# Four attention layers: which score banks VectorE takes over from ScalarE, by quota or by backlog

## The chip, the cores and the metric

The kernel runs on one core of one Trainium2 chip. The time is device microseconds of one execution; the number to compare is the median of several runs. Profiles are single executions taken by the hardware profiler, and a profile's times are measured from the first instruction of its span.

## What is computed

Four layers in a row on x of 2048 positions by 640 features, all bf16. Layers 0 and 2 use the weights A and attend to a sliding window of 256 positions; layers 1 and 3 use the weights B and attend to all 2048 positions. There are 32 heads of 20 features.

```python
x = x + A(layernorm(x)); x = x + B(layernorm(x))     # layers 0, 1
x = x + A(layernorm(x)); x = x + B(layernorm(x))     # layers 2, 3
# A, B: qkv = x @ wqkv; p = softmax(q k^T / sqrt(20)) (A: only 0 <= i - j < 256)
#       return (p v) @ wo
```

## The kernel before

**Units and banks.** The queries come in 4 chunks of 512 positions, the heads in 8 groups of 4. A unit is one layer, one chunk, one group (class Unit, L696). A full-attention unit has 16 key blocks of 128 times 4 heads, 64 score banks; a bank is a 128 x 512 block of scores (keys by queries) in one PSUM bank. A windowed unit has 12 banks. The first chunk of layer 1 is cut into parts of 4 key blocks, that of layer 3 into one of 12 and one of 4 (PARTS), since the last keys of a layer exist only when the layer before it is done. The list `units` (L752 on) fixes the order: layer 0 with the parts of layer 1's first chunk woven in; then layer 1's chunks 1 to 3 with the windowed units of layer 2's chunks 0 to 2 between them; then layer 3's first chunk, 12 key blocks a unit, with the windowed units of layer 2's last chunk after its fourth unit; then the 4 remaining key blocks of that chunk, 16 banks a unit; then layer 3's chunks 1 to 3.

**The main loop** (from L1323) goes tile by tile. A tile is 3 banks, sometimes 2 or 4, held alternately in PSUM banks 0 to 2 and 3 to 6. TensorE computes its scores (L1359), ScalarE takes the exponential of the whole tile in one instruction (L1387) and writes it to `pt` in SBUF; two or three tiles later TensorE multiplies it by the values into PSUM bank 7 (L1420). At a unit's end VectorE copies bank 7 out (finish_unit, L861; copies at L869, L871, L883, L885), and a tail task normalizes it (t_tail, L1065). In windowed units masks are multiplied in by VectorE (L1474) and by GpSimd (L1463).

**Background tasks** (layer norm, projections, output projection, tails) are generators in an ordered list. pump() advances them by a credit for each tile. They use PSUM banks 5 and 6, later bank 6 alone (take_m, L273); a task in the midst of a bank holds it (`state["held"]`). When TensorE would have too little to do, keep_clock (L663) adds filler matmuls on the masks (L307).

**VectorE's own exponentials.** Some score banks are not given to ScalarE. VectorE turns them into exponentials by arithmetic on the bits of the number. The bank is read from PSUM into a 32-bit integer form (side_fixed, L947; instruction L957). Two such banks make a pair, for which t_chain (L965) issues four more VectorE instructions (L969, L978, L980, L982). There are two buffers `xi` for the integer form, and three (layer 1) or five (layer 3) for the result, which stay taken until TensorE has multiplied the pair by the values (side_values, L1004; matmul L1010). In layer 1 these buffers lie in `raw_o` (side_early, L919), in layer 3 in buffers of the normalized input `xnT` and in `ka` and `qa` (side_start, L906).

Which banks are put aside is fixed when the units are made (put_aside, L683): in layers 1 and 3 from chunk 1 on, the last banks of each unit, 4 in layer 1, 6 or 8 by turns in layer 3, 4 in the very last unit, none in unit (3, 1, 0). In layer 1 a moved bank sits as the third bank of a tile, at fixed places written into the list `tiles` before the loop starts (L1252 to L1277), so that tile gives ScalarE 2 banks. In layer 3 it goes to PSUM bank 6 beside a full tile (side_scores, L937; scores L944), when `side_now` says so: no task holds bank 6, the bookkept backlog is under LAG = 0.5, the unit that the bank belongs to was loaded at least 8 tiles ago.

**The backlog.** `state["lag"]` is a running account, in microseconds, of the work issued to VectorE and not yet done: each VectorE operation adds a written-down cost (0.6 for a copy out of PSUM in evac, 1.2 in stats, 0.7 for L957, 0.7, 0.7, 1.2 and 1.2 for the steps of a chain), and each tile takes off its columns divided by 1200, plus 0.05 (L1447), that is 1.33 for 3 banks and 0.90 for 2. After each tile, side_work (L990) issues further steps of the chains while the account is under WORK = 1.0. Where a unit ends before its pairs are done, side_done (L1030) forces the steps out.

Of the kernel before, what the change touches and what calls it, by code (L numbers as in the profile page):

```python
# [23 lines left out]
NT = S // P  # L24
# [15 lines left out]
LAG = 0.5  # L40
WORK = 1.0
SIDE_1 = 4
SIDE_3 = (6, 8)
# [9 lines left out]
def kernel(  # L53
# [272 lines left out]
    def evac(out_, in_):  # L326
        if state["act"]:
            nc.scalar.copy(out=out_, in_=in_)
        else:
            state["lag"] += 0.6  # L330
            nc.vector.tensor_copy(out=out_, in_=in_)  # L331
# [60 lines left out]
    def stats(l, c, i):  # L392
        if (l, c) not in mvs:
            mvs[l, c] = lnp.tile([P, 4, 2], F32, name="mv", tag="mv")
        state["lag"] += 1.2
        st = lnp.tile([P, 2, 6], F32, name="stats", tag="stats")
        xv = x_sb[:, 4 * c + i, :]
        nc.vector.bn_stats(out=st[:, 0, :], in_=xv[:, 0:HD])
        nc.vector.bn_stats(out=st[:, 1, :], in_=xv[:, HD:D])
        nc.vector.bn_aggr(out=mvs[l, c][:, i, :], in_=st[:])  # L400
# [282 lines left out]
    def put_aside(l, c, g):  # L683

        if l == 1:
            n = SIDE_1
        else:
            n = 4 if (c, g) == (NC - 1, G - 1) else SIDE_3[g % 2]
        if n == 2:
            return ((NT - 1, 2), (NT - 1, 3))  # L690
        return tuple((NT - 1 - i // 4, i % 4) for i in range(n))

# [3 lines left out]
    class Unit:  # L696
        def __init__(self, l, c, g, part=None):
            self.l, self.c, self.g, self.part = l, c, g, part
            self.windowed = l % 2 == 0
            self.aside = ()  # L700
            if self.windowed:
                sets = [(m, b0, subs, j) for m, b0, subs in window_banks(c) for j in range(4)]
            else:

                if c > 0 and (l, c, g) != (3, 1, 0):
                    self.aside = put_aside(l, c, g)
                k0, k1 = key_blocks(l, part)
                sets = [
                    (None, 0, [(kc, 0, 4, 0)], j) for kc in range(k0, k1) for j in range(4)
                    if (kc, j) not in self.aside  # L710
                ]
            n = len(sets)
            self.banks = [
                (self, j, m, b0, subs, i < 4, i >= n - 4 + len(self.aside), i == n - 1)
                for i, (m, b0, subs, j) in enumerate(sets)
            ]
# [144 lines left out]
    def finish_unit(u):  # L861
# [31 lines left out]
    side_todo = deque(  # L893
        (u, p, i) for u in units for p in range(len(u.aside) // 2) for i in range(2)
    )
    side_left = Counter({id(u): len(u.aside) for u in units})
    side_out = {}
    side = {"xi": deque(), "chain": deque(), "out": deque(), "late": False}
# [7 lines left out]
    def side_start():  # L906

        assert live["xnT"] == 0 and not side["chain"] 
        tl = [xtp.tile([P, KD, C], BF16, name="xnT", tag="xnT") for _ in range(3)]
        live["xnT"] += 3  # L910
        f = [v[:, 0:4, :].rearrange("p a b -> p (a b)").bitcast(F32) for v in tl]
        side["xi"].clear()
        side["out"].clear()
        outs = [ka_all[:, KA - 6 + 2 * n : KA - 4 + 2 * n, :] for n in range(3)]
        outs += [qa_all[:, 2 * n : 2 * n + 2, :] for n in range(2)]
        side_tiles(f[0:2], f[2].bitcast(F16)[:, 0 : 2 * C], outs)
        side["late"] = True
# [9 lines left out]
    def side_free():  # L927

        if not side_todo or not side["late"]:
            return False  # L930
        u, p, i = side_todo[0]
        return (
            id(u) in loaded and state["tick"] >= loaded[id(u)] + 8
            and mfree[6][0] <= state["tick"] and (i == 1 or len(side["xi"]) > 0)
        )

    def side_scores():  # L937

        u, p, i = side_todo[0]
        mseq[0] += 1  # L940
        mfree[6] = (state["tick"] + 2, mseq[0])
        kc, j = u.aside[2 * p + i]
# [4 lines left out]
    def side_fixed(z):  # L947

        u, p, i = side_todo.popleft()
        side_left[id(u)] -= 1  # L950
        if not side_left[id(u)] and id(u) in deferred:
            live["kt"] -= 1
            live["qt"] -= 1
        if i == 0:
            side["now"] = side["xi"].popleft()
        xi = side["now"]
# [33 lines left out]
    def side_work(force):  # L990

        while (force or state["lag"] < WORK) and side["chain"]:
# [11 lines left out]
    def side_values(u, pairs, done):  # L1004

        for n in range(done, len(pairs)):
            pt = pairs[n][0]
            for i in range(2):
                kc, j = u.aside[2 * n + i]
                nc.tensor.matmul(  # L1010
                    op[32 * j : 32 * j + VW, :], lhsT=u.v(kc, j), rhs=pt[:, i, :], start=False,
                    stop=all(jj != j for _, jj in u.aside[2 * n + i + 1 :]),
                    skip_group_check=True,
                )
            side["out"].append(pt)

    def side_push():
# [3 lines left out]
        if side_free():  # L1021
            side_scores()
# [7 lines left out]
    def side_done(u):  # L1030

        n = 0
        while len(side_out.get(id(u), ())) < len(u.aside) // 2:
            n += 1
            assert n < 10000
            side_push()
        return side_out.pop(id(u))
# [5 lines left out]

    def s_emitted(u):
# [6 lines left out]
        elif side_left[id(u)]:  # L1051
# [187 lines left out]
    with tc.manual_schedule():  # L1239
# [11 lines left out]
        banks = [b for u in units for b in u.banks]  # L1251
        tiles = []  # L1252
        starts = {}
        n = 0
        last_layer = sum(len(u.banks) for u in units[: index[3, 1, 0, None]])
        placed = {}
        while n < last_layer:
            size = 2 if len(tiles) % 2 and narrow(banks[n][0]) else 3
            u = banks[n][0]
            at = placed.setdefault(id(u), [])  # L1260
            extra = []
            if (
                len(at) < len(u.aside) and banks[n + 1][0] is u
                and len(tiles) >= (15 // (SIDE_1 - 1) if SIDE_1 > 2 else 3) * len(at) + (at or [0])[0]
            ):
                kc, j = u.aside[len(at)]
                extra = [(u, j, "side", 0, [(kc, 0, 4, 0)], False, False, False)]
                at.append(len(tiles))
                size = 2
            for b in banks[n : n + size]:  # L1270
                starts.setdefault(id(b[0]), len(tiles))
            tiles.append(banks[n : n + size] + extra)
            n += size
        for m, b in enumerate(banks[n:]):
            starts.setdefault(id(b[0]), len(tiles) + m // 3)
        banks = deque(banks[n:])

        side_now = False

        def next_tile(t):  # L1280

            if t < len(tiles):
                return tiles[t]
            size = 3
            if side_now:
                return [banks.popleft() for _ in range(min(size, len(banks)))]
            if t % 2 and not tails and state["held"] is None and mfree[6][0] < state["tick"]:
                if all(task.wake > state["tick"] for task in todo) :
                    size = 4
            return [banks.popleft() for _ in range(min(size, len(banks)))]  # L1290

        def rate(t):

            if t >= len(tiles):
                return 0.45
            u = tiles[t][0][0]
            if index[u.l, u.c, u.g, u.part] < woven:
                return 1.2
            done, r = 0.0, 0.6 if state["early"] else 0.3
            for task in todo:  # L1300
                done += max(task.left, 0.0)
                if task.need < len(units):
                    r = max(r, done / max(starts[id(units[task.need])] - t - 16, 1))
# [10 lines left out]
        last_tick[0] = len(tiles)  # L1314
# [4 lines left out]
        valued = 0  # L1319
# [4 lines left out]
        while ended is None or t < ended + 8:  # L1324
# [3 lines left out]
            if t < len(tiles) or banks:  # L1328
                if t >= len(tiles) and not side["late"] and not live["xnT"] and not todo:
                    side_start()  # L1330
                side_now = (
                    state["held"] is None and state["lag"] < LAG and side_free()
                )
                cur = next_tile(t)
# [28 lines left out]
                if cur[-1][2] == "side":  # L1363
                    cur = cur[:-1]
                    n_b -= 1
                    if "early" not in side:
                        side_early()
                    while not side_todo[0][2] and not side["xi"]:
                        assert side_work(True)
                    side_fixed(sp[:, n_b, :])  # L1370
                if side_now:
                    side_scores()
# [28 lines left out]
            for n in range(2 if n_b == 0 or t > closed + 1 else 0):  # L1401
# [15 lines left out]
                for m, (kc, q0, qn, col) in enumerate(subs):  # L1417
                    for _, pg, i, b in group:
# [4 lines left out]
                            start=(first and m == 0), stop=(last and m == len(subs) - 1),  # L1423
                            skip_group_check=u.windowed or len(u.aside) > 0,
                        )
                if first:
                    valued = 0
                if u.aside and not end:
                    pairs = side_out.get(id(u), ())
                    if len(pairs) > valued and pairs[valued][1] + 3 <= state["tick"]:  # L1430
                        if valued + 1 < len(u.aside) // 2:
                            side_values(u, pairs[: valued + 1], valued)
                            valued += 1
                if end and u.aside:
                    side_values(u, side_done(u), valued)
# [87 lines left out]
```

## Time and profile before

| | before |
|---|---|
| median of 3 runs | 2195.17 us (2189.13 to 2195.78) |
| the profiled execution | 2197.81 us |
| its span, first to last instruction | 2196.1 us |
| granted TensorE clock over the span | 0.993 |
| ScalarE, exponentials (L1387) | 1646 instructions, 2072.1 us busy |
| VectorE, banks read for its own exponentials (L957) | 96 in layer 1, 158 in layer 3 |

In the profile, PE is TensorE, PEld its weight loads, DVE is VectorE, ACT is ScalarE, POOL is GpSimd, SP the engine that issues most DMAs. L957 is line 957 of the kernel. A group's line gives the line, the engine and operation, what it writes and reads by the program's names with shapes, the count, then busy time and mean time of one, then the idle time of the engine just before, with what ended it. A row on waits names the instruction that waited, what it waited for, and the total, the number and the longest of these waits.

### The profile page before, as it was taken

Reading aid. Unit: us, or ns where it says so; the run is one execution under the profiler, and the core shown is the slowest. Engines: PE = TensorE matmul, PEld = TensorE weight load, DVE = VectorE, ACT = ScalarE, POOL = GpSimd, SP = SyncE. Lnnn points to the kernel's source line nnn. Section 1 sums busy time; section 2 is a strip of 40 time slices with the busy share of each in tenths; the row PEclk is TensorE's granted clock in tenths of the full one; section 3 lists DMA queues with packets and bytes.
Section 4 is the critical chain, followed back from the end, with each engine's and each line's share of the span. In section 5 each row is a group of like instructions: output and inputs, shape, how many; then the busy total and the mean of one; then the engine's idle time right before and its main releaser. Section 6 shows DMA issues by size and latency. Waiting matters only on the chain. (4 is left out here: it accounts for less than half of the span.)

```text
span 2196.1 us, 73000 instructions
## 1 busy us (share of the span) xinstructions
PE 1931.1 (88%) x31782; PEld 760.4 (35%) x31783; DVE 1324.3 (60%) x2308; ACT 2112.9 (96%) x1726; POOL 483.3 (22%) x952
## 2 busy tenths in 40 slices
PE   8999998988889888888888988888888988888887
PEld 3444443433333333333333433342222222222222
DVE  5556565425656666566665743532487778778873
ACT  7789899999999999999999999999999999999997
POOL 6665556110121113401143112511000000000000
PEclk9899999999999999999999999999999999999999
DMA  6223233322210323112231123122112111111100
GB/s 201 74 82 107 68 98 99 81 78 64 74 46 27 83 60 90 39 37 64 64 101 34 35 86 98 39 57 65 48 43 61 32 32 41 35 32 35 53 20 17
DMA packets 88416, 137.27 MB, mean 63 GB/s; under 512 B 20766, under 2 KB 63486, under 8 KB 88094
## 3 DMA queue, kind: packets, MB, share of 16 engines
q1 hardware_dynamic: 68878, 79.43, 13.1%
q0 software_dynamic: 19216, 53.17, 8.2%
q8 instruction: 249, 4.08, 0.8%
q14 instruction: 73, 0.60, 0.1%
HBM read 99.52 MB, written 27.79 MB: 58 GB/s over the span
## 5 line engine op out<-in xcount | busy, mean ns | idle before, releaser
L1387 ACT ACTIVATE pt<-ps 128x1536 bf16<-128x1536 f32 (+2 forms) x1646 | 2072.1, 1438 | 46.1 <-PE ps L1359 36.1
L1359 PE MATMUL ps<-qt,kt 32*128 32x512 bf16 x3938 | 542.4, 384 | 79.3 <-ACT pt L1387 70.2
L307 PE MATMUL ps<-masks,ident 128*32 128x512 bf16 x5676 | 504.6, 387 | 99.4 <-ACT pt L1387 54.8
L1420 PE MATMUL ps<-pt,vt 128*21 128x512 bf16 x3826 | 383.1, 387 | 1.1 <-issue 1.1
L1359 PEld LDWEIGHTS <-kt 32*128 32x128 bf16 x3938 | 161.0, 91 | 482.7 <-issue 461.0
L307 PEld LDWEIGHTS <-ident 128*32 128x32 bf16 x5676 | 179.9, 94 | 283.1 <-issue 254.7
L1463 POOL TENSOR_SCALAR_AFFINE_SELECT pt<-pt 128x256 bf16<-128x256 bf16 (+2 forms) x505 | 213.2, 444 | 184.4 <-ACT pt L1387 181.8
L307 PE MATMUL ps<-xnT,wqk 128*32 128x512 bf16 x3320 | 224.8, 381 | 12.4 <-DVE on L1128 2.8
L331 DVE CAST st<-ps 128x512 bf16<-128x512 f32 x134 | 92.7, 691 | 169.1 <-PE ps L307 164.9
L1420 PEld LDWEIGHTS <-vt 128*21 128x21 bf16 x3842 | 95.0, 89 | 254.9 <-issue 251.5
L957 DVE TENSOR_SCALAR xnT<-ps 128x512 int32<-128x512 f32 x158 | 109.2, 691 | 109.2 <-PE ps L944 108.4
L307 PE MATMUL ps<-wop,on 128*32 128x320 bf16 x3712 | 160.9, 300 | 6.8 <-DVE x_sb L579 3.3
L1474 DVE TENSOR_TENSOR pt<-pt,masks 128x512 bf16<-128x512 bf16 (+4 forms) x267 | 111.3, 433 | 61.3 <-ACT pt L1387 59.8
L307 PEld LDWEIGHTS <-on 128*32 128x32 bf16 x5760 | 122.2, 95 | 66.6 <-issue 33.6
L1359 PE MATMUL ps<-qa,ka 32*128 32x384 bf16 (+2 forms) x1408 | 114.5, 278 | 24.4 <-ACT pt L1387 21.2
L307 PE MATMUL ps<-wv,xnT 128*32 128x320 bf16 x2560 | 116.6, 302 | 7.9 <-DVE on L1128 3.3
L579 DVE TENSOR_TENSOR x_sb<-x_sb,ps 128x320 bf16<-128x320 bf16 x120 | 58.3, 486 | 105.8 <-PE ps L307 104.9
L307 PEld LDWEIGHTS <-wqk 128*32 128x32 bf16 x3320 | 83.5, 96 | 95.9 <-issue 38.0
L1128 DVE TENSOR_TENSOR on<-on,ps 128x512 bf16<-128x512 bf16 x128 | 86.3, 683 | 47.8 <-PE ps L307 46.9
L885 DVE CAST on<-ps 128x512 bf16<-128x512 f32 x112 | 77.1, 688 | 61.7 <-PE ps L1010 36.1
L957 DVE TENSOR_SCALAR raw_o<-ps 128x512 int32<-128x512 f32 x96 | 66.1, 689 | 61.4 <-PE ps L1359 60.3
L546 POOL DMA_DIRECT2D k_d<-st x75 | 42.6, 568 | 224.2 <-DVE st L331 209.1
(101 smaller groups left out, 1638.5 us busy)
## 6 DMA issues: line engine op xcount, KB each, us to landing
vt<-v_d SPq DMA_DIRECT2D x48, 336.0 KB
kt<-k_d SPq DMA_DIRECT2D x192, 80.0 KB
wqk<-in_B_wqkv_dram POOLq DMA_DIRECT2D x80, 160.0 KB, 3.5
wqk<-in_A_wqkv_dram POOLq DMA_DIRECT2D x70, 160.0 KB, 3.5
k_d<-st POOLq DMA_DIRECT2D x75, 128.0 KB, 2.3
q_d<-st POOLq DMA_DIRECT2D x75, 128.0 KB, 2.1
qt<-q_d SPq DMA_DIRECT2D x384, 20.0 KB
v_d<-vs POOLq DMA_DIRECT2D x16, 336.0 KB, 3.1
```

The costliest lines, as they stand in the source:

```text
L307: nc.tensor.matmul(out_[r], lhsT=lhsT[:, r], rhs=rhs, start=start, stop=stop)
L331: nc.vector.tensor_copy(out=out_, in_=in_)
L546: nc.gpsimd.dma_start(out=dst, in_=staging.pop())
L579: nc.vector.tensor_tensor(out=xv, in0=had, in1=yp, op=ALU.add)
L885: nc.vector.tensor_copy(out=oT, in_=op)
L957: nc.vector.tensor_scalar(out=xi.bitcast(I32)[:, i * C : (i + 1) * C], in0=z, scalar1=SCALE * LOG2E * FIX, scalar2=127.5 * FIX, op0=ALU.mu ...
L1128: nc.vector.tensor_tensor(out=oT, in0=oT, in1=zb, op=ALU.mult)
L1359: nc.tensor.matmul(sp[:, i, col * P : (col + qn) * P], lhsT=u.k(kc, j), rhs=u.q(j, q0, qn), start=True, stop=True,)
L1387: nc.scalar.activation(out=pt[:, i:k, b0 * P :], in_=sp[:, i:k, b0 * P :], func=ACT.Exp, scale=SCALE,)
L1420: nc.tensor.matmul(op[32 * j : 32 * j + VW, q0 * P : (q0 + qn) * P], lhsT=u.v(kc, j), rhs=pg[:, i, col * P : (col + qn) * P], start=(first ...
L1463: nc.gpsimd.affine_select(out=v, in_=v, compare_op=ALU.is_gt if later else ALU.is_ge, fill=0.0, base=0, pattern=[[0, k - i], [-1 if later ...
L1474: nc.vector.tensor_tensor(out=pt_[:, i:k, cols], in0=pt_[:, i:k, cols], in1=mv_, op=ALU.mult)
```

## The change

The fixed quotas go (put_aside, SIDE_1, SIDE_3, the prepared list of tiles). Units keep their banks in a queue `rest`, and the loop takes them as it goes. Before each tile it asks side_giver for a unit that gives a bank, if the backlog is under LAG (0.5) in layer 3 or LAG_1 (0.3) in layer 1. The giver is the first of up to three units, in order, that is loaded for 8 tiles and has at least 30 banks left if it has begun, or 12 if it has not; it gives its last banks, two by two. Chain steps are issued under WORK (1.0) in layer 3 and WORK_1 (0.7) in layer 1. Layer 3's first chunk may give banks too: its buffers are taken as soon as the last windowed unit is past, at most one `xnT` is live and no `qa` or `ka` is, where before they were taken at the start of chunk 1. The pairs' values are multiplied as they come ready. Three weights of the account change. MOST_1 = 64 is no smaller than a unit. The core of the diff:

```diff
+LAG_1 = 0.3
+WORK_1 = 0.7
+KEEP = 30
+MOST_1 = 64
-SIDE_1 = 4
-SIDE_3 = (6, 8)
...
-            state["lag"] += 0.6
+            state["lag"] += 0.7 if in_.shape[-1] == C else 0.5
...
-        state["lag"] += 1.2
+        state["lag"] += 1.1
...
+    givers = [u for u in units if not u.windowed and (u.l, u.c) != (1, 0)]
...
+    def side_giver():
+        if side["half"] is not None:
+            return side["half"][0]
+        if not side["xi"]:
+            return None
+        while side["at"] < len(givers) and not givers[side["at"]].rest:
+            side["at"] += 1
+        for n in range(side["at"], min(side["at"] + 3, len(givers))):
+            u = givers[n]
+            if id(u) not in loaded or state["tick"] < loaded[id(u)] + 8:
+                return None
+            if not side["late" if u.l == 3 else "early"]:
+                return None
+            if u.l == 1 and len(u.aside) >= MOST_1:
+                continue
+            if len(u.rest) >= (KEEP if len(u.rest) + len(u.aside) < u.size else 12):
+                side["at"] = n
+                return u
+        return None
...
-        while (force or state["lag"] < WORK) and side["chain"]:
+        while (force or state["lag"] < (WORK if side["late"] else WORK_1)) and side["chain"]:
...
+            if state["unit"] < final:
+                size = 2 if t % 2 and narrow(flow[0]) else 3
+                if giver is None or giver.l == 3 or size == 2:
+                    return take(size)
+                kc, j = side_take(giver)
+                return take(2) + [(giver, j, "side", 0, [(kc, 0, 4, 0)], False, False, False)]
...
-                if t >= len(tiles) and not side["late"] and not live["xnT"] and not todo:
+                if (
+                    not side["late"] and state["unit"] >= index[3, 0, 4, PARTS[3][0]]
+                    and live["xnT"] <= 1 and not live["qa"] and not live["ka"]
+                ):
                     side_start()
...
+                giver = side_giver() if state["lag"] < (LAG if side["late"] else LAG_1) else None
+                if giver is not None and giver.l == 3 and (
+                    state["held"] is not None or mfree[6][0] > state["tick"]
+                ):
+                    giver = None
+                cur = next_tile(t, giver)
```

## Prediction

> **What bounds the kernel now.** I read the engine table of the page first, then the busy time by stage, then what ScalarE waited for in each stage, then its instructions by shape.
>
> ```profile
> PE 1931.1 (88%) x31782; PEld 760.4 (35%) x31783; DVE 1324.3 (60%) x2308; ACT 2112.9 (96%) x1726; POOL 483.3 (22%) x952
> ```
>
> ScalarE is 96% busy and VectorE 60%, so an exponential that VectorE does instead is worth ScalarE's time for it, as long as VectorE is not late. The busy time by stage is more telling. The columns are window, its length, then PE, PEld, DVE, ACT and POOL with counts, the granted clock, DMA:
>
> ```profile
> 500.00:1287.00 787.00, 688.24 (x11541) 282.03 (x11538) 492.79 (x867) 774.29 (x625) 174.51 (x326) 1.00 0.22 60
> 1287.00:1420.00 133.00, 115.15 (x2057) 48.62 (x2057) 56.07 (x119) 131.93 (x100) 49.12 (x97) 1.00 0.26 71
> 1420.00:1562.00 142.00, 120.67 (x1940) 48.62 (x1940) 39.56 (x83) 141.72 (x107) 15.89 (x24) 0.99 0.22 61
> 1562.00:2160.00 598.00, 530.35 (x7061) 164.65 (x7061) 455.41 (x594) 593.89 (x440) 0.00 (x0) 1.00 0.13 37
> 2160.00:2196.00 36.00, 27.16 (x324) 10.79 (x325) 10.89 (x27) 24.32 (x19) 0.00 (x0) 0.95 0.06 20
> ```
>
> I chose the cuts by the units' closing copies (L883, L885, L869): stage 1 is layer 1's chunks 1 to 3 with layer 2's chunks 0 to 2 between them; stage 2 is layer 3's first chunk up to its fourth unit, with layer 2's last chunk; stage 3 is the rest of that first chunk; stage 4 is chunks 1 to 3 of layer 3; stage 5 is the end. ScalarE is 98 to 100% busy in stages 1 to 4. VectorE is 63% busy in stage 1, 42% in stage 2, 28% in stage 3, 76% in stage 4. What ScalarE waited for in stage 1, then in stage 4 (total us, times, longest):
>
> ```profile
> ACT pt L1387 <- PE ps L1359: 11.0, 28, 0.9
> ```
>
> ```profile
> ACT pt L1387 <- PE ps L1359: 2.3, 9, 0.4
> ```
>
> So these stages last as long as ScalarE's exponentials do, within 2%. A bank less on ScalarE is time off the end.
>
> **What a bank is worth.** ScalarE's exponentials in stage 1 by shape (busy us, mean ns of one):
>
> ```profile
> L1387 ACT ACTIVATE pt<-ps 128x1536 bf16<-128x1536 f32 x486 | 673.0, 1534 | 12.0 <-PE ps L1359 11.0
> L1387 ACT ACTIVATE pt<-ps 128x1024 bf16<-128x1024 f32 x103 | 113.7, 1112 | 0.1
> ```
>
> Successive ones overlap, so I take the distance from start to start in the trace: median 1.331 us after a 3-bank tile and 0.905 us after a 2-bank one, means 1.360 and 1.008. A bank taken out of a tile is thus worth 0.426 us by the medians and 0.352 us by the means. The means hold what TensorE makes ScalarE wait behind a short tile, so I use 0.352 in stage 1. In layer 3 the bank is not taken out of a tile; tiles stay 3 banks wide and fewer are needed, so a bank is worth a third of the mean tile there, 1.360/3 = 0.453 us.
>
> **What a bank costs VectorE.** The chain now, whole run:
>
> ```profile
> L957 DVE TENSOR_SCALAR xnT<-ps 128x512 int32<-128x512 f32 x158 | 109.2, 691 | 109.2 <-PE ps L944 108.4
> L957 DVE TENSOR_SCALAR raw_o<-ps 128x512 int32<-128x512 f32 x96 | 66.1, 689 | 61.4 <-PE ps L1359 60.3
> ...
> L982 DVE SCALAR_TENSOR_TENSOR raw_o<-raw_o 128x1024 uint16<-128x1024 int32 x48 | 58.6, 1221 | 0.9
> L980 DVE SCALAR_TENSOR_TENSOR raw_o<-raw_o 128x1024 f16<-128x1024 f16 x48 | 58.5, 1220 | 0.9
> ...
> L969 DVE TENSOR_SCALAR raw_o<-raw_o 128x1024 f16<-128x1024 int16 x48 | 33.2, 691 | 0.8
> L978 DVE TENSOR_TENSOR raw_o<-raw_o 128x1024 f16<-128x1024 f16 x48 | 32.9, 686 | 0.8
> ```
>
> L957 counts the banks moved: 96 in layer 1, 158 in layer 3, 254 in all. A pair costs 2 x 0.69 + 0.69 + 0.69 + 1.22 + 1.22 = 5.20 us, 2.60 us a bank. The change leaves this chain as it is. All that counts is how many banks the new rule moves, where, and what it makes wait.
>
> **Stage 1: the quota of 4 goes, the backlog decides.** VectorE's 492.8 us hold 96 x 2.60 = 250 us of chains, so 243 us are other work. The nearest row for a free-running backlog rule is stage 4: there a bank is taken whenever the bookkept backlog is under 0.5 and bank 6 is free, and its pairs follow each other every 5 to 9 us with no longer gap up to 2145 us, so its quota hardly binds and its 76% is what such a rule reaches. 76% of 787 is 598 us; less 243 leaves 355, or 137 banks. But stage 1's bars are lower (0.3 for a bank, 0.7 for a chain step against 1.0), which costs slots: with nothing else queued a pair takes two 2-bank tiles and then four 3-bank tiles with one step each, 2 x 0.905 + 4 x 1.331 = 7.1 us for 5.2 us of work, and any other copy of 0.7 takes a tile's step. Carrying the bookkeeping tile by tile with the other work where it now lies gives 132. I take 130, 34 more: 34 x 0.352 = **12.0 us**. Bounds: none more (96, if the low bar starves the rule), and 85% of VectorE, 669 - 243 = 426, 164 banks, 68 more and 24 us.
>
> **Stage 2: nothing.** Layer 3's banks may only be given once the large buffers are free, after the last windowed unit, and layer 1 has none left.
>
> **Stage 3 takes part.** The buffers are taken once at most one normalized chunk is live and no windowed query or key is. The casts of the projections (L331 st) before 1376 us hold every block of layer 3's first three chunks, and the last windowed unit closes at 1418.5, so it starts near 1420 instead of 1567 us, where the first L957 of layer 3 lies now. 76% of 142 us less the 39.6 of other work leaves 68 us, 26 banks. Up to 1516 us, though, tasks hold PSUM bank 6, which a score bank needs too. I take 20: 20 x 0.453 = **9.1 us**. Bounds: 8 banks (the quiet 46 us from 1516 to 1562 alone, less about 15 us for the eight closings there, at a pair in 7.3 us) to 26; 3.6 to 11.8 us.
>
> **Stage 4 stays.** Its bars are the same. It now moves a pair in 7.3 us (79 pairs from 1567 to 2145), paced by the bars and by bank 6, which is blocked for two tiles after each. **The end:** the last unit's quota ran out at 2145 us; now it gives until 30 banks of it are left, some 11 tiles after it starts at 2159, to about 2174. That is 29 us, 4 pairs; I take 6 banks as closing tasks use bank 6: 6 x 0.453 = **2.7 us**, between 0 and 3.6.
>
> **What costs nothing.** The new weights of the backlog (0.7 or 0.5 for 0.6, 1.1 for 1.2) shift which tile is chosen; that is in the count. Value matmuls of the moved banks only change place (L1010 for L1420), so TensorE, 87% busy in stage 1, has the same work in less time. Part of that is filler that keeps its clock (L307 on masks), which covers 24 us; without it the short tiles would cost what the mean of 1.008 already shows. No DMA is added or moved.
>
> **Sum.** 12.0 + 9.1 + 2.7 = 23.8 us, from 60 banks (254 to 314). The profiled execution took 2197.81 us (span 2196.1), so it would take 2174.0. The median of the runs shown, 2195.17, is 2.6 lower; from it the change gives 2171.4. I say 2171.
>
> **Rivals.** Times are from the median.
> *The low bar starves stage 1.* If each copy of 0.5 or more costs a slot, layer 1 keeps about 96 banks and only 11.8 us come in: 2183. For it: 579 of the stage's 867 instructions are other work. Against: its 96 now go through with gaps of 1 to 2 us before most L957.
> *Stage 1 fills further.* At 85% of VectorE, 24 + 9.1 + 2.7 = 36 us: 2159. For it: the stage's 294 us of idle VectorE. Against: stage 4 does not get past 76%.
> *Nothing new is moved*, because taking from the end of a unit keeps the buffers waiting for its values: 254 banks, 2195. Against: the three pair buffers of layer 1 come free within the unit that gave them.
> *Masks held up.* In stage 1 part of the windowed masks run on GpSimd (L1463, median 0.41 us for two banks); none of the 240 after 480 us overlaps a chain step with two SBUF operands (L978, L980, L982). If a step holds the mask behind it, 17 more pairs hold it for up to 17 x 1.22 = 21 us, TensorE's values wait, and the gain shrinks to 3 us: 2192. Against: values follow their exponentials by three tiles, and the 0.45 booked for each of VectorE's masks keeps the rule from choosing there. [...]
> *Slower: the last chunk's projections come late.* In stage 3 score banks now share bank 6 with the tasks that make layer 3's last keys (first cast 1477 us; the units that need them start at 1503). The tiles there also end some 9 us sooner. If the tasks slip by more than about 10 us, each of the eight 16-bank units starts on its own load, seen once on the chain that ended last (start, us):
>
> ```profile
> 1553.34 3.14 DMA vt<-v_d
> 1556.50 2.03 DMA kt<-k_d
> ```
>
> That is 5.2 us each, TensorE and then ScalarE behind it. From five such units the gain is gone; all eight cost 41 us, 2195 + 41 - 24 = 2212. Against: the tasks' order puts these keys first, and ten casts in 40 us leave TensorE filler.
>
> **How the numbers follow.** Forecast 0.56, starved 0.12, fuller 0.12, nothing new 0.05, masks 0.04, slower 0.11. About 0.3% (6.6 us) can be told from no change. Faster is 0.56 + 0.12 + 0.12 = 0.80; within 0.3%, 0.05 + 0.04 = 0.09; slower 0.11. The range runs from 2153, about the fuller case with 0.426 us a bank in stage 1 (68 x 0.426 + 11.8 = 40.8), to 2194, over the masks' case, and leaves out the slower case and part of no change.
>
> **What would show it.** In the profile after, L957's successor counts some 130 on raw_o and 184 on xnT, the latter from about 1425 us on. Layer 1's stage is 12 us shorter with VectorE near 75%, ScalarE still at 98%. 1536-wide exponentials fall by about 34 + 9. If ScalarE's wait for scores in stage 1 grows from 11 us to over 20, the bank is worth less than I took. If layer 1's count is far from 130, my slots are wrong; waits for vt or kt near 1490 to 1550 us show the slower rival.

## The result, and the profile after

The changed kernel takes 2223.7 us (median of 4 runs, 2222.97 to 2227.55) against 2193.0 us for the kernel before beside it: a ratio of 1.0145, 95% interval 1.0123 to 1.0167. It is slower by 31 us, where a gain of 24 us was forecast. The profiled execution took 2223.22 us, its span 2221.5 us.

The engine table of the page after, then the two groups of VectorE's own exponentials (L976 is L957 of before):

```profile
PE 1948.6 (88%) x31906; PEld 758.5 (34%) x31907; DVE 1487.9 (67%) x2508; ACT 2091.2 (94%) x1716; POOL 496.9 (22%) x954
...
L976 DVE TENSOR_SCALAR xnT<-ps 128x512 int32<-128x512 f32 x186 | 128.5, 691 | 130.3 <-PE ps L960 129.0
...
L976 DVE TENSOR_SCALAR raw_o<-ps 128x512 int32<-128x512 f32 x134 | 91.8, 689 | 34.3 <-PE ps L1381 28.1
```

320 banks are moved, 66 more than before, and ScalarE is 22 us less busy. That is what the change is for. Yet the kernel is longer, so ScalarE now waits. The busy time by stage, cut at the same closing copies as before (window, length, PE, PEld, DVE, ACT, POOL, clock, DMA):

```profile
495.00:1289.00 794.00, 693.04 (x11566) 280.77 (x11558) 587.12 (x982) 762.42 (x625) 186.03 (x327) 1.00 0.22 59
1289.00:1421.00 132.00, 114.17 (x2013) 47.63 (x2007) 56.40 (x120) 131.99 (x99) 49.85 (x97) 1.00 0.26 71
1421.00:1591.00 170.00, 138.23 (x2095) 52.50 (x2088) 94.66 (x150) 132.76 (x98) 16.56 (x24) 0.94 0.19 50
1591.00:2187.00 596.00, 527.36 (x7047) 163.11 (x7043) 459.45 (x601) 592.10 (x438) 0.00 (x0) 1.00 0.13 37
2187.00:2222.00 35.00, 26.70 (x339) 10.49 (x337) 19.82 (x38) 23.47 (x18) 0.00 (x0) 0.96 0.06 21
```

Two stages carry the loss. Stage 3 is 170 us long instead of 142, though ScalarE is 9 us less busy in it. Stage 1 is 794 instead of 787, though ScalarE is 12 us less busy. To the tenth, from the closing copies of the two profiles: the part up to stage 1 is 5.3 us shorter, stage 1 is 7.0 longer, stage 2 0.3 shorter, stage 3 27.5 longer, the rest 3.3 shorter. The first part's 5.3 us are within the spread of single profiles: the kernel before with one constant changed in layer 1 (the sixth run below) also closes layer 0 nearly 4 us sooner than the profile of before, and the eleven variants of the changed kernel below, which are alike up to there, reach stage 1 at 492 to 498 us.

What ScalarE waited for in stage 1, then in stage 3:

```profile
ACT pt L1405 <- PE ps L1381: 24.8, 57, 1.8
```

```profile
ACT pt L1405 <- PE ps L1381: 36.6, 11, 30.7
```

In stage 1 there are twice as many waits as before (57 for 28), none over 2 us. In stage 3 a single wait of 30.7 us is more than the whole loss of that stage. ScalarE's timeline there shows it (start, length, idle before in brackets):

```profile
1495.73 2.79 ACT L1405 ACTIVATE pt<-ps 128x1536 bf16<-128x1536 f32 x2 [1.07 <-PE ps L1381]
1529.24 2.79 ACT L1405 ACTIVATE pt<-ps 128x1536 bf16<-128x1536 f32 x2 [30.72 <-PE ps L1381]
```

And the chain that ended last, from 1498 to 1523 us and on, shows what was done meanwhile (start, us):

```profile
1512.48 1.55 PE ps L309 x20
1514.05 0.51 DVE vs L333
1514.60 1.46 PE ps L309 x20
1516.08 0.50 DVE vs L333
1516.62 0.89 PE ps L309 x20
1517.54 0.50 DVE vs L333
```

```profile
1522.30 0.70 DVE st L333
1523.29 2.23 DMA k_d<-st
1527.73 1.57 DMA kt<-k_d
```

This is the last chunk's norm, values and first key block, bank after bank, one engine waiting for the other, then the key's way through memory. The first 16-bank unit needs them, so the schedule ran these tasks at once (`require`) before its first score. In the kernel before the same casts were done at 1456 to 1477 us, beside tiles, and the unit found them ready. The tasks began late: the output projection's eight adds before them lie at 1460 to 1495 us, before at 1430 to 1451.

### The profile page after: what moved, and what is told of

Read it like the earlier page. It is cut to its first block, busy times and chain, and to the rows that moved or that the text cites. A ratio compares the mean times of both kernels' runs of the same rounds, so it can differ in the third digit from the quotient of the medians.

```text
span 2221.5 us, 73408 instructions
## 1 busy us (share of the span) xinstructions
PE 1948.6 (88%) x31906; PEld 758.5 (34%) x31907; DVE 1487.9 (67%) x2508; ACT 2091.2 (94%) x1716; POOL 496.9 (22%) x954
## 5 line engine op out<-in xcount | busy, mean ns | idle before, releaser
L1405 ACT ACTIVATE pt<-ps 128x1536 bf16<-128x1536 f32 (+3 forms) x1636 | 2050.4, 1402 | 98.0 <-PE ps L1381 83.4
L309 PE MATMUL ps<-masks,ident 128*32 128x512 bf16 x5800 | 512.0, 386 | 105.3 <-ACT pt L1405 56.6
L1438 PE MATMUL ps<-pt,vt 128*21 128x512 bf16 x3760 | 377.0, 386 | 1.0 <-ACT pt L1405 1.0
L1381 PEld LDWEIGHTS <-kt 32*128 32x128 bf16 x3910 | 152.7, 91 | 474.1 <-issue 445.4
L1476 POOL TENSOR_SCALAR_AFFINE_SELECT pt<-pt 128x128 bf16<-128x128 bf16 (+2 forms) x507 | 226.1, 470 | 189.7 <-ACT pt L1405 151.1
L309 PE MATMUL ps<-xnT,wqk 128*32 128x512 bf16 x3320 | 227.2, 384 | 13.7 <-DVE st L333 2.4
L976 DVE TENSOR_SCALAR xnT<-ps 128x512 int32<-128x512 f32 x186 | 128.5, 691 | 130.3 <-PE ps L960 129.0
L1487 DVE TENSOR_TENSOR pt<-pt,masks 128x256 bf16<-128x256 bf16 (+4 forms) x269 | 117.8, 450 | 33.4 <-ACT pt L1405 31.9
L309 PE MATMUL ps<-wv,xnT 128*32 128x320 bf16 x2560 | 119.0, 307 | 16.8 <-DVE vs L333 8.7
L976 DVE TENSOR_SCALAR raw_o<-ps 128x512 int32<-128x512 f32 x134 | 91.8, 689 | 34.3 <-PE ps L1381 28.1
L415 POOL TENSOR_SCALAR rstd<-mv 128x4 f32<-128x4 f32 x15 | 5.2, 348 | 421.8 <-DVE mv L402 421.5
```

The lines of the kernel that those rows point to most:

```text
L309: nc.tensor.matmul(out_[r], lhsT=lhsT[:, r], rhs=rhs, start=start, stop=stop)
L976: nc.vector.tensor_scalar(out=xi.bitcast(I32)[:, i * C : (i + 1) * C], in0=z, scalar1=SCALE * LOG2E * FIX, scalar2=127.5 * FIX, op0=ALU.mu ...
L1381: nc.tensor.matmul(sp[:, i, col * P : (col + qn) * P], lhsT=u.k(kc, j), rhs=u.q(j, q0, qn), start=True, stop=True,)
L1405: nc.scalar.activation(out=pt[:, i:k, b0 * P :], in_=sp[:, i:k, b0 * P :], func=ACT.Exp, scale=SCALE,)
L1438: nc.tensor.matmul(op[32 * j : 32 * j + VW, q0 * P : (q0 + qn) * P], lhsT=u.v(kc, j), rhs=pg[:, i, col * P : (col + qn) * P], start=(first ...
L1476: nc.gpsimd.affine_select(out=v, in_=v, compare_op=ALU.is_gt if later else ALU.is_ge, fill=0.0, base=0, pattern=[[0, k - i], [-1 if later ...
```

## The experiments

Twelve kernels, each compared with the kernel before on the same chip. "Stage 1" below is the time in that run's profile from the last closing copy of layer 1's first chunk to that of unit (1, 3, 7). For three profiles with the same code in stage 1 it came out as 780, 784 and 785 us, and for four others as 792 to 795, so it is good to some 3 us.

**1. No banks in stage 3.**

```diff
-                    not side["late"] and state["unit"] >= index[3, 0, 4, PARTS[3][0]]
-                    and live["xnT"] <= 1 and not live["qa"] and not live["ka"]
+                    not side["late"] and state["unit"] >= final
+                    and not live["xnT"] and not todo
```

> The changed kernel, but layer 3's large buffers are taken where the kernel before takes them, at the start of its chunk 1, so no bank of stage 3 is moved; 134 banks in layer 1 as in the changed kernel, 166 in layer 3. Theory A (almost all of the loss is the stall in stage 3, where the score banks hold back the last chunk's projections): stage 3 goes from 170 us back to about 142, and the kernel takes about 2223.7 - 28 = 2196 us, still not faster than before, since stage 1 lost 7 us. Rival B (the loss is spread over the kernel): above 2210 us.

2197.5 us, ratio 1.003 (1.002 to 1.004). Stage 3 is back at 142.8 us, and ScalarE does not wait there at all. Theory A is right to 2 us: some 25 of the 31 us lost come from the banks in stage 3, and what is left is a small loss still.

**2. Four banks a unit in layer 1, on top of that** (MOST_1 = 4).

> As the run with stage 3 off, and each unit of layer 1 gives 4 banks at most, so 96 there as before instead of 134. Theory A (the 38 further banks of stage 1 give ScalarE's time back in waits): stage 1 is not slower with 96 than with 134, about 787 us against 794, and the kernel takes about 2190 us. Rival B (each further bank is worth 0.352 us as predicted, and something else costs stage 1 its time): 13 us longer than with 134, about 2209 us.

2208.1 us, 1.0076 (1.0059 to 1.0092); stage 1 804 us. Theory A fell, the rival's 2209 was met. The 38 banks between 96 and 134 are worth 804.3 - 791.7 = 12.6 us, 0.33 each, close to the 0.352 of the prediction. So 96 banks chosen by backlog cost 17 us more than 96 by quota (804.3 against 786.9): not their number but something in the way in which the new rule moves them costs the time.

**3. Stage 3's banks in their tiles**, not in PSUM bank 6.

```diff
-                if giver is None or giver.l == 3 or size == 2:
+                if giver is None or size == 2:
...
-                if giver is not None and giver.l == 3 and (
+                if giver is not None and state["unit"] >= final and (
                     state["held"] is not None or mfree[6][0] > state["tick"]
```

> The changed kernel, but in stage 3 a moved bank is the third bank of its tile, as in layer 1, instead of lying in PSUM bank 6; 26 banks there. Theory A (the projections were late because score banks took bank 6 from the tasks): tasks keep bank 6, the stall of 30 us goes, stage 3 takes 142 - 26 x 0.352 = 133 us, and the kernel about 2223.7 - 37 = 2187 us. Rival B (they were late because VectorE had too much to do): the stall stays over 15 us, and the kernel takes over 2205 us.

2194.2 us, 1.0007 (0.9997 to 1.0018). VectorE has more to do than in the changed kernel (26 banks for 22), and the stall is gone; the output projection's adds lie at 1431 to 1453 us. So it was the place in bank 6, not VectorE's load. But stage 3 takes 140.3 us, 2.5 less than with no bank moved, where 9 were expected: ScalarE waits 5.8 us there, and a bank brought 0.1 us.

**4. Layer 1's bars as high as layer 3's**, without stage 3 (LAG_1 = 0.5, WORK_1 = 1.0).

> As the run with stage 3 off, with layer 1's bars at layer 3's (0.5 for a bank, 1.0 for a chain step instead of 0.3 and 0.7): 164 banks in layer 1 instead of 134. Theory A (more banks make VectorE late, TensorE waits for it and ScalarE for TensorE): stage 1 is 5 to 10 us longer than with 134, the kernel about 2203 us. Rival B (a bank is worth 0.352 us whatever the bar): 30 x 0.352 = 11 us shorter, about 2185 us.

2216.8 us, 1.0116 (1.0101 to 1.0131), 19 us slower than with 134 banks; theory A had the sign, with a third of the size. Stage 1 takes 817 us. ScalarE's idle time there grows by 33 us (its waits for scores are 54.2 us in all, single ones up to 3.2), three times the 11 us that the 30 banks should give.

To see where the waits lie I counted, in the traces, ScalarE's idle time in the first and the second tile behind each 2-bank exponential. "Close" is how many of these have the next one within two tiles:

| kernel | 2-bank tiles | close | idle 1st, 2nd, later, us | stage 1, us |
|---|---|---|---|---|
| before | 103 | 4 | 4.3, 5.9, 2.6 | 786.9 |
| after | 132 | 65 | 19.7, 6.4, 5.5 | 793.9 |
| 1, no stage 3 | 132 | 65 | 18.8, 6.4, 4.6 | 791.7 |
| 2, four a unit | 94 | 49 | 13.8, 8.4, 5.1 | 804.3 |
| 4, bars up | 170 | 77 | 32.2, 21.6, 8.7 | 817.1 |
| 5, spacing 4 | 127 | 2 | 7.0, 9.2, 5.0 | 785.1 |
| 6, quota in a row | 102 | 74 | 19.5, 0.3, 3.5 | 799.4 |
| 7, short chain | 132 | 65 | 16.4, 3.4, 4.9 | 785.4 |
| 9, light | 132 | 64 | 7.5, 9.3, 28.1 | 808.8 |
| 10, light, spacing 4 | 123 | 3 | 0.1, 1.1, 20.3 | 785.8 |

The quota put a bank into every fifth tile. The backlog rule puts half of them one or two tiles apart. Hence theory S, and the runs that follow.

**5. At least four tiles between moved banks in layer 1**, without stage 3.

```diff
+                if giver is not None and giver.l == 1 and t - side["last"] < 4:
+                    giver = None
                 cur = next_tile(t, giver)
```

> As the run with stage 3 off, and in layer 1 two moved banks lie at least 4 tiles apart; 124 banks there, at the same bars. Theory S (ScalarE's waits come from 2-bank tiles that follow each other within one or two tiles): ScalarE's waits in stage 1 fall from 29 us to about 13, as in the kernel before (0.1 us per short tile), stage 1 takes 787 - 28 x 0.42 = 775 us, and the kernel about 2181 us. Rival Q (the waits follow from the number of banks that VectorE has taken): 124 is nearly 134, stage 1 stays near 792 us and the kernel at 2196 to 2201 us.

2186.7 us, 0.9981 (0.9972 to 0.9991), 10.8 us less than without the spacing, with ten banks fewer. Rival Q is out. Theory S has the sign and the place (idle in the first tile 18.8 to 7.0), not the size: its 2181 was missed.

**6. The quota itself, in four successive tiles**: the kernel before with one constant changed.

```diff
-                and len(tiles) >= (15 // (SIDE_1 - 1) if SIDE_1 > 2 else 3) * len(at) + (at or [0])[0]
+                and len(tiles) >= 1 * len(at) + (at or [0])[0]
```

> The kernel before, with its quota of 4 banks in layer 1 put into four successive tiles at the start of each unit instead of every fifth tile; 96 banks as before, nothing else changed. Theory S: stage 1 is 10 to 17 us longer, the kernel takes 2201 to 2208 us. Rival Q (number, not place) or a rival that puts the loss on another part of the new rule: 2191 us as before.

2206.5 us, 1.0067 (1.005 to 1.0084), as theory S expected. This is the plainest of the twelve: the same 96 banks, the same code, no new rule, and 15 us lost. ScalarE's waits in its stage 1 (before: 11.0, 28, 0.9):

```profile
ACT pt L1387 <- PE ps L1359: 21.0, 49, 1.0
```

**7. Less for VectorE, the same choice.** Two of the four chain steps are not issued but still booked, so the polynomial of the moved banks' exponentials is left out in part.

```diff
-        V.tensor_tensor(out=q, in0=t, in1=t, op=ALU.mult)
         yield 0.7
-        V.scalar_tensor_tensor(out=q, in0=q, scalar=TB, in1=t, op0=ALU.add, op1=ALU.mult)
         yield 1.2
...
-            out=po.bitcast(U16), in0=xi.bitcast(I32), scalar=1.0 / C, in1=q,
+            out=po.bitcast(U16), in0=xi.bitcast(I32), scalar=1.0 / C, in1=t,
```

> As the run with stage 3 off, every tile and every bank chosen as there, but two of the four steps of each chain on VectorE are left out (the square and the product, 0.69 and 1.22 us), so that the moved banks get wrong exponentials and VectorE has 128 us less to do in stage 1. Theory V (ScalarE waits because VectorE is late with its copies out of bank 6, and TensorE behind it): ScalarE's waits in stage 1 fall from 29 us to under 18, the kernel takes about 2185 us. Theory T (two short tiles in a row are too short for TensorE's own work): the waits stay above 25 us and the time near 2197 us.

2185.2 us, 0.9976 (0.9965 to 0.9988): the time is theory V's. The waits are not: 24.7 us of idle time, the first tile still at 16.4. Inconclusive as to shares. VectorE's load costs something like 6 us (by stage 1) to 12 us (by the whole kernel, where layer 3's chains are shorter too) in this arrangement, and it is not the main thing that makes the first tile behind a short one late.

**8. Spacing of 4 in stages 1 and 3, stage 3's banks in their tiles** (the edits of 3 and 5, the spacing's condition `state["unit"] < final`).

> The changed kernel with moved banks in stage 3 as the third bank of their tile, and at least 4 tiles between moved banks in stages 1 and 3; 124 and 20 banks. Theory S: stage 1 about 775 us, stage 3 about 143 - 20 x 0.42 = 135 us, the kernel about 2173 us, faster than both. Rival Q: 2190 us or more.

2181.9 us, 0.9959 (0.9946 to 0.9972). Faster than both, but 9 us short of theory S. Stage 3 takes 144.5 us, 1.7 more than with no bank moved. Part of the gain falls behind it: ScalarE has ten banks fewer left to do there, and the rest of the kernel takes 626.0 us against 631.2 in run 5. Together the 24 more banks of layer 3 (190 for 166) bring 3.5 us, 0.15 each.

**9. Nothing but values behind a short tile.**

```diff
+            if n_b == 2 and index[1, 1, 0, None] <= state["unit"] < final:
+                return
             state["least"] = (1.76 if state["unit"] >= woven else 1.0) * n_b / 3
```

> As the run with stage 3 off, bars and choice unchanged (banks may follow each other), but behind a 2-bank tile no background task is advanced and no filler issued, so TensorE has only the values between its scores and the next tile's; 126 banks in layer 1, as the tasks shift. Theory T (a task's burst of up to 1.26 us or filler behind a short tile makes TensorE late, since ScalarE needs 0.905 us for it): ScalarE's waits in stage 1 fall from 29 us to under 15, stage 1 from 792 to about 780 us, the kernel to about 2186 us. Theory V (VectorE's lateness, whatever TensorE has): the waits stay above 24 us, the kernel at 2196 us or, with less time for the tasks, above.

2212.5 us, 1.0094 (1.0065 to 1.0123): both theories missed it. Behind a short tile theory T is borne out, 18.8 us of idle time become 7.5. But the tasks and chains now fall due elsewhere, the idle time in later tiles grows from 4.6 to 28.1 us, 12 of it where TensorE waits for a moved pair whose chain is not done. Something else changed with it, which neither theory named: the granted clock of TensorE is at half for 55 us of stage 1, in run 1 for none, and 14 us of ScalarE's idle time lie in those stretches. Whether the missing filler or the longer waits brought the clock down is open (run 4, with all its filler but with waits as long, has 38 us at half). The rows of stage 1, run 1's and run 9's (the clock is the third number from the end, 1.00 and 0.97):

```profile
493.00:1285.00 792.00, 691.77 (x11567) 281.04 (x11567) 587.00 (x983) 762.27 (x625) 186.05 (x327) 1.00 0.22 59
497.00:1302.00 805.00, 690.49 (x11073) 279.98 (x11072) 562.10 (x951) 760.05 (x622) 180.32 (x321) 0.97 0.21 57
```

**10. The same with spacing and stage 3 in tiles.**

> The run with 4 tiles between moved banks and stage 3's in their tiles, also with no task and no filler behind a 2-bank tile; 120 and 20 banks. Theory T: waits in stage 1 fall from 21 us to about 10, stage 1 to about 776 us, the kernel to about 2171 us. Theory V, or tasks that come late when 140 tiles give them nothing: 2182 us or more.

2188.9 us, 0.9992 (0.9978 to 1.0006), 7 us slower than run 8. The idle time in the two tiles behind a short one is all but gone (0.1 and 1.1 us), and 20.3 us have appeared later on. So the wait behind a short tile is TensorE's task or filler; taking both from there saved nothing. Stage 1 is 2.2 us longer than run 8's by the profiles, the rest of the difference lies behind it. Here too the clock is at half for longer, 27 us of stage 1 against 10 in run 8, with 8 us of the idle time in it, so work that is put off and a slower clock are not told apart. A run that leaves out the tasks and keeps the filler was not made.

**11. The changed kernel, bank 6 left to the tasks** (`or state["unit"] < final and (todo or tails)` added to the condition that drops a giver).

> The changed kernel, with score banks again in PSUM bank 6 in stage 3, but none while any background task or tail is listed; 4 banks there instead of 22. Theory A (the score banks in bank 6 hold the tasks back, and the stall is the last chunk's projections done at once with nothing beside them): first output-projection add of stage 3 near 1430 instead of 1460 us, no wait of ScalarE over 5 us, stage 3 about 142 us, the kernel about 2196 us. Rival (the early taking of the buffers itself delays the tasks, since three of the five buffers of the normalized input are gone): a wait of 10 us or more stays, over 2206 us.

2200.7 us, 1.0044 (1.0028 to 1.006). No stall, the first add at 1434.6 us, so theory A holds and the early taking of buffers is harmless. It is 4.7 us over the number, and one wait shows why (ScalarE's part of it is 5.2 us, where none over 5 was expected): a pair's second bank was held back while tasks were listed, and at the unit's end TensorE waited for its chain.

```profile
PE ps L1031 <- DVE ka L1001: 4.8, 1, 4.8
```

**12. Spacing of 4, and stage 3 only from its 16-bank units on, in tiles.**

> At least 4 tiles between moved banks in layer 1 and in stage 3, stage 3's in their tiles and only from its 16-bank units on, where the last chunk's keys are done; 124 and 6 banks. Theory S with A: stage 1 as in the run with spacing (785 us), stage 3 about 141 us, the kernel 2180 to 2184 us, faster than both kernels by 0.3 to 0.5%. If the 20 banks of stage 3 were what made the run with spacing in both stages faster: 2187 us.

2180.9 us (median of 6), 0.9955 (0.9942 to 0.9969), as expected, though not by the sum alone. It is 5.8 us under run 5, and six banks give 6 x 0.453 = 2.7 us at most; the profiles put 5.0 us into stage 1 (780.2 against 785.2), where the code is the same and the granted clock was at half for 13.7 us in run 5 and for none here. With run 8 it is the fastest of all; the two can't be told apart.

## Why the prediction was wrong, point by point

**What bounds the kernel: right, and too narrow.** ScalarE does set the time of stages 1 to 4. But "a bank less on ScalarE is time off the end" holds only while TensorE delivers the next tile in the shorter time, and TensorE was 87% busy in the same row.

**The count of banks: right.** Forecast 130 in layer 1 and 184 in layer 3, 20 of them in stage 3; 134, 186 and 22 came. VectorE is 74% busy in stage 1, as said. Two readings behind it were off without harm: by the trace the pairs of stage 4 lie up to 10.3 us apart, not 5 to 9, and in layer 1 46 of the 96 L957 had a gap before them, not most.

**What a bank is worth: this step failed in stage 1.** The prediction took 0.352 us from the mean 2-bank tile of before, which "hold what TensorE makes ScalarE wait behind a short tile". Those were 103 short tiles, 99 of them more than two tiles from the next. The step carried their price over to a rule that places them where VectorE is idle, often in neighbouring tiles, though the prediction itself worked out the cycle (two 2-bank tiles, then four of 3 banks) from which the neighbours follow. The term was mis-sized by that: from start to start ScalarE takes 1.135 us on the mean behind a 2-bank tile after, 1.008 before (3-bank tiles 1.369 and 1.361). For 132 such tiles that is 16.8 us, most of the 19 us between the forecast 12.0 shorter and the measured 7.0 longer. With about the same share of neighbours (65 of 132 and 49 of 94 close) a further bank is worth what was said (0.33 us, runs 1 and 2). The placing alone costs 12.5 us for 96 banks (run 6: 799.4 against 786.9), out of the 17 us by which the backlog's 96 were slower than the quota's (run 2); the other 5 us are not traced to one part of the new rule. ScalarE's exponentials after, in stage 1, show both sides at once; before, 486 and 103 had 12.0 and 0.1 us of idle time before them:

```profile
L1405 ACT ACTIVATE pt<-ps 128x1536 bf16<-128x1536 f32 x452 | 624.3, 1491 | 25.8 <-PE ps L1381 20.2 <-PE ps L1438 2.1 <-POOL pt L1476 1.6
L1405 ACT ACTIVATE pt<-ps 128x1024 bf16<-128x1024 f32 x133 | 137.9, 1070 | 5.0 <-PE ps L1381 4.6
```

Busy time fell by 12 us, as forecast; idle time rose by 19. The claim that less filler would cover TensorE ("filler that keeps its clock, which covers 24 us") failed with it. The filler did not shrink: in stage 1 it took 162.7 us before and 165.0 after. And it and a task's bank are issued whole, up to 1.26 us at a time, where a 2-bank tile leaves 0.905 us.

**Stage 3: this step failed too; the slower rival was the case, at 0.11.** The sum had 9.1 us of gain here, and the stage came out 27.5 us longer. The rival's place (the last chunk's projections), cause (bank 6) and point (a slip of more than 10 us) were named; the slip was 30 us at the first add. The weighing was wrong in two ways. "Tasks hold PSUM bank 6" was read as a limit on the score banks; in the code the giver is asked before the tasks are pumped, so whenever the account is under 0.5 a score takes the bank for two tiles, and the tasks get it only in between. And the rival's price was taken from a load seen on the chain, 5.2 us for each unit. In truth the tasks themselves were due: everything from the norm to the first key in one piece, 30.7 us, once. The 22 banks gave some 22 x 0.453 = 10 us there, against which the stall of 30.7 and 6 us of smaller waits stand.

**Stage 4 and the end: right.** 164 banks for 158, 3.3 us shorter, forecast 2.7. **Stage 2: right**, nothing. **Masks held up: it happened, and was small.** Before, none of GpSimd's 240 masks after 480 us overlapped a chain step; after, 29 of 242 do, and they take longer (the last section has the numbers). But ScalarE's waits on GpSimd's masks in stage 1 are 2.2 us in all, too small to matter.

**What stays open.** With the waits behind short tiles gone (run 10) ScalarE still idles as much as in run 5, in later tiles: I have not found an arrangement in which 28 or 38 more banks of layer 1 bring their 0.35 us. Spacing 4 (three profiles, mean 783 us) is 4 us better than before for 28 banks, 0.14 each, and the one profile of before makes that uncertain by some 3 us. There the time behind a 2-bank tile is back at 1.00 to 1.01 us, but 3-bank tiles take 1.371 to 1.380, 1.361 before; with 457 of them that is 5 to 9 us. How much of this is VectorE's lateness (run 7), how much the bunching of tasks on TensorE and how much TensorE's clock is not settled.

## What to carry to other kernels

A mean duration of a short piece of work on the bounding engine holds for the spacing at which it was measured; before pricing more of them, look at how far apart the new rule puts them and what the engine behind has to do in between. A choice by backlog looks at one engine's account only: here it took neither TensorE's burst nor the shared PSUM bank into account, and an even quota beat it with fewer banks. When optional work shares a buffer with work that has a due time, ask who gets the buffer first, and price a miss as the whole of the late work done with nothing beside it, not as its last load.

## What the runs showed of the hardware

The stall was lengthened a little by TensorE's clock. In the 31 us of the stall (the profile after) the granted clock is 0.73 on the mean, with TensorE 16.4 us busy:

```profile
1498.00:1529.00 31.00, 16.43 (x275) 8.88 (x275) 8.70 (x18) 0.52 (x1) 6.24 (x10) 0.73 0.30 70
```

The trace has it at 0.5 from 1502.1 to 1515.8 us, and again from 1526.0 to 1532.9. In the chain above, 20 matmuls of a values bank take 1.55 us up to 1514 and 0.89 us from 1516.6 on, 0.66 us more for each of the first four banks and 0.57 for the fifth: 3.2 us of the 30.7. The Trainium skill (TensorE: Matmul & The Clock Gate, Part 1: The HAM clock gate) says that the array falls to half its clock after a window of about 3.4 us in which it was idle. The second fall agrees: TensorE did nothing in the 3.4 us before it. The first does not: in the 3.4 us before 1502.1 TensorE was busy for 1.1 us, and its longest pause was 2.9 us. So the first fall came without an idle window of that length; what set it off is not shown.

GpSimd's masks took longer where they overlapped a VectorE instruction with two operands in SBUF. In the profile after, the 29 that overlap such a chain step (L997, L999, L1001) take 0.62, 0.69 and 0.97 us on the median for 128, 256 and 384 columns, up to 1.62; masks that overlap nothing on VectorE take 0.29, 0.41 and 0.52. In the profile before, 120 of the 240 overlap one of VectorE's own mask products (L1474, two such operands as well), and those of 128 and 256 columns take 0.38 and 0.52 us instead of 0.29 and 0.40. No mask that overlaps neither takes over 0.54 us in either profile. Spans on GpSimd are rough, and no run varied this alone, so the overlap is shown and the reason is not.
